# The order of the first unit's convolution, and more matmuls on zeros ahead of it

## The chip, the cores and the metric

The kernel runs on one core of one Trainium2 chip. A core has five engines that work side by side and wait for each other by semaphores: TensorE (PE, matrix products into the PSUM memory), VectorE (DVE), ScalarE (ACT), GpSimd (POOL) and SyncE (SP, which here only issues transfers). The metric is the device time of one execution in microseconds. The runs of the kernel before took 705.57 us in the median of three (705.44 to 706.24).

## The reference

```python
def _attn_ref(x, weight):             # x: (8, 4096, 192), weight: (8 heads, 7 taps)
    w = np.exp(weight - weight.max(-1, keepdims=True))
    w = w / (w.sum(-1, keepdims=True) + 1e-09)
    x_pad = np.concatenate([zeros(B, 6, 192), x], axis=1)
    x_unf = x_pad[:, idx, :].reshape(B, S, 7, 8, 24)      # idx[s, k] = s + k
    return np.einsum('hk,bskhg->bshg', w, x_unf).reshape(B, S, 192)

def _moe_ref(x, w_in, w_out):         # x: (32768, 192), w_in: (192, 2048), w_out: (2048, 192)
    h = x @ w_in
    return (h * np.cos(h)) @ w_out
```

So each token's 192 channels are first smoothed over the last seven tokens, with seven weights per head (24 channels each) that a softmax makes, and then go through a layer of 2048 hidden values with g = h cos h between two matrix products. Output and inputs are float32; the kernel multiplies in bfloat16 and adds up in float32.

## The kernel before, in words

The 32768 tokens are handled in units of 1024 tokens and tiles of 512 (two tiles a unit, 64 tiles). For a tile, the first product (`mm1`, L504) makes two blocks of 128 hidden values at a time in a PSUM tile `h` of two banks, eight times; ScalarE takes the cosine (L511), VectorE multiplies (L515) into `g`, and the second product (`mm2_step`, L553) adds 64 steps up in two PSUM banks `o_ps`. Three PSUM tiles `h` form a ring (`h_pool`), which the convolutions of the start use as well (`ring_banks`, `o_bank`). The order of TensorE's work within each tile is written out by hand (`PE_FIRST`, `PE_ORDER`), in program order per engine; an engine runs its instructions in that order and waits where an input is missing. The second product of tile 0 starts with the first `m1` in `PE_FIRST[0]`, after four of the eight `h` steps, `d11` and `h5`, `c11` (the convolution of unit 1 by a band matrix). `W0` and `W1` cast the two halves of w_out to bfloat16 on GpSimd (`cast_wo`, L123).

The first unit is convolved in another way, since nothing is at hand yet. Its eight blocks of 128 tokens form four pairs. `cast_first` (L396) casts two blocks of x. `turn_pair` (L406) turns one pair on TensorE with the identity matrix: six matmuls of 128 columns and six of 6 columns, so that channels lie on the partitions and tokens along the row; a copy takes the result to `xT`. `conv_pair` (L415) then adds up seven taps: for each tap j two matmuls, on the two halves of the rows, of a matrix that has the tap's weight on its diagonal (`diag`, made by `make_diag` from `wn`) with `xT` shifted by j tokens, 384 columns each. `conv_copy` (L424) takes one half of the result to `cT`, the left-hand input of the first product. Pairs 2 and 3 are convolved later, between the first products (`conv_later`, `v2` and `v3` in `PE_FIRST[0]`).

Around the change, the orders are these. TensorE: matmuls on zeros (`keep_warm`, 3 of them, L169), the weight's broadcast (L172), `WARM[0]` zeros (L173), the pick matmuls (L443), pair 0 turned (L444), `WARM[1]` zeros, pair 1 turned (L447), pair 0 convolved (L460), pairs 2 and 3 turned (L464), pair 1 convolved (L466), then the first product. ScalarE: casts of x, a table load for the sine, the copy of the turned pair 1, another cast, a copy of convolved pair 0, the copy of turned pairs 2 and 3, a copy of convolved pair 1. VectorE: the copy of turned pair 0, diagonals, `prod`, a copy of pair 0, `bands` (L468), a copy of pair 1. GpSimd: loads of w_in (L113, two early, two at L452), one cast of x, then 16 copies that put `bands` into the band matrix (L481), which unit 1's convolution needs, then unit 1's cast (L219) and w_out's.

SP's queue: unit 0 in three loads at the start; then a nop (L473) that waits for `m`, the second copy of pair 0 (VectorE's); behind it unit 1 in two loads (L103), its edges (L88), w_out in four loads (L127), then unit 2. So none of these is issued before `m` is done.

Of the kernel before, what the change touches and what calls it, by code (L numbers as in the profile page):

```python
# [16 lines left out]
def kernel(  # L17
# [8 lines left out]
    nc = tc.nc  # L26
# [5 lines left out]
    T = 512  # L32
# [9 lines left out]
    NC = D // 64  # L42
# [13 lines left out]

    CW = 2 * NPB * OP

    WARM, OUT = (2, 1), ((0, 1), (0, 1))
    xf = x.rearrange("b s d -> (b s) d")  # L60

    consts = ctx.enter_context(tc.tile_pool(name="consts", bufs=1))
# [72 lines left out]
    zero = consts.tile([128, T], BF16)  # L135
# [11 lines left out]
    nc.vector.memset(band, 0.0)  # L147
    idle = o_pools[0].tile([128, T], FP32, name="o_ps0")

    def keep_warm(n, bank=idle):  # L150
        for _ in range(n):
            nc.tensor.matmul(out=bank, lhsT=zero[:, 0:128], rhs=zero, start=True, stop=True)  # L152


    nc.gpsimd.affine_select(out=head, in_=head, compare_op=ALU.not_equal, fill=-1.0, base=0,
# [6 lines left out]
                          in_=bass.AP(ident.tensor, ident.offset, [ident[0:64].ap[0], [R, HQ], [HQ * R, 4], [0, 32]]))  # L162
# [4 lines left out]
    scrap = consts.tile([128, 1], FP32)  # L167
    nc.scalar.activation(out=scrap, in_=one, func=AF.Exp)
    keep_warm(3)  # L169
    w_all = o_pools[1].tile([128, T], FP32, name="o_ps1")  # L170
    w_bc = w_all[:, 0:K]
    nc.tensor.matmul(out=w_bc, lhsT=head, rhs=w_row, start=True, stop=True)  # L172
    keep_warm(WARM[0])  # L173

    wmax = consts.tile([128, 1], FP32)
# [65 lines left out]
    def ring_banks():  # L241
        h = h_pool.tile([128, 2, T], FP32, name="h")
        return [h[:, 0, :], h[:, 1, :]]
# [146 lines left out]
    EDGE = K - 1  # L390
    copies = [nc.scalar.copy, nc.vector.tensor_copy]
    cT[0] = cT_pool.tile([128, NC * (UB + 1) * 128], BF16, name="cT")
    xT = consts.tile([128, UB // 2, NC, EDGE + 128], BF16)
    diag = consts.tile([128, K, 2, 64], BF16)

    def cast_first(n0, n1, copy):  # L396
        copy(out=xb0[:, :, n0 + 1 : n1 + 1, :].rearrange("p k n m -> p n k m"),
             in_=x_tiles[0][:, n0:n1, :].rearrange("p n (m k) -> p n k m", k=NC))

    def make_diag(j0, j1):  # L400
        nc.vector.tensor_tensor(
            out=diag[:, j0:j1].rearrange("p j t m -> p j (t m)"),
            in0=double.rearrange("p (o t) m -> p o (t m)", o=1).to_broadcast([128, j1 - j0, 128]),
            in1=wn[:, j0:j1].rearrange("p (j o) -> p j o", o=1).to_broadcast([128, j1 - j0, 128]), op=ALU.mult)

    def turn_pair(p, ps):  # L406
        to = ps[:, 0 : NC * (EDGE + 128)].rearrange("p (k t) -> p k t", k=NC)
        for k in range(NC):
            for prev, t0, t1 in ((0, EDGE, EDGE + 128), (1, 0, EDGE)):
                n = 2 * p + 1 - prev  # L410
                nc.tensor.matmul(out=to[:, k, t0:t1], lhsT=xb0[:, k, n : n + 2, :].rearrange("p n m -> p (n m)"),  # L411
                                 rhs=ident[:, 128 - (t1 - t0) : 128], start=True, stop=True, skip_group_check=True)
        return to

    def conv_pair(p, ps, j0=0, j1=K):  # L415
        for j in range(j0, j1):
            for i in range(2):
                rows = slice(64 * i, 64 * i + 64)
                nc.tensor.matmul(out=ps[i][:, 0 : NC * 128].rearrange("p (k t) -> p k t", k=NC),  # L419
                                 lhsT=diag[rows, j].rearrange("p t m -> p (t m)"), rhs=xT[rows, p, :, j : j + 128],  # L420
                                 start=j == 0, stop=j == K - 1, skip_group_check=True)
        return ps

    def conv_copy(p, i, ps, copy):  # L424
        m = NC * (2 * p + i)
        return copy(out=cT[0][:, m * 128 : (m + NC) * 128], in_=ps[i][:, 0 : NC * 128])  # L426
# [10 lines left out]
    def o_bank(b):  # L437
        return o_pools[b].tile([128, T], FP32, name="o_ps%d" % b)
# [3 lines left out]
    for i in range(HQ):  # L442
        nc.tensor.matmul(out=wb[:, K * i : K * i + K], lhsT=pick[:, i], rhs=wn[0:64], start=i == 0, stop=i == HQ - 1, skip_group_check=True)  # L443
    to = [turn_pair(0, ring_banks()[0])]  # L444
    keep_warm(WARM[1])
    cast_first(2, 4, nc.scalar.copy)
    to.append(turn_pair(1, ring_banks()[0]))  # L447
    make_diag(0, 4)
    nc.vector.tensor_copy(out=xT[:, 0], in_=to[0])
    nc.scalar.activation(out=scrap, in_=one, func=AF.Sin)  # L450
# [8 lines left out]
                            in1=wb[:, 0 : HQ * K].rearrange("p (h o k) -> p h o k", o=1, k=K).to_broadcast([128, HQ, E, K]), op=ALU.mult)  # L459
    ps0 = conv_pair(0, [o_bank(0), ring_banks()[0]])  # L460
    conv_copy(0, 0, ps0, copies[0])
    m = conv_copy(0, 1, ps0, copies[1])
    rest = ring_banks()
    to = [turn_pair(2 + i, rest[i]) for i in range(2)]  # L464
    nc.scalar.copy(out=xT[:, 2:4], in_=bass.AP(to[0].tensor, to[0].offset, [to[0].ap[0], [T, 2], [1, NC * (EDGE + 128)]]))
    ps1 = conv_pair(1, [ring_banks()[0], o_bank(1)])  # L466
    bands = consts.tile([128, HQ, E], FP32)
    nc.vector.tensor_reduce(out=bands, in_=prod, axis=mybir.AxisListType.X, op=ALU.add)  # L468
    nc.gpsimd.tensor_copy(out=tap, in_=wn)
    conv_copy(1, 0, ps1, copies[0])  # L470
    conv_copy(1, 1, ps1, copies[1])

    tc.add_manual_dep(nc.sync.nop().ins, m.ins.name, sync_dep, reason="order of the transfers")  # L473
    load_unit(1, 0, NB)
# [4 lines left out]
    for i in range(16):  # L479
        q, rows = divmod(i, 4)  # L480
        nc.gpsimd.tensor_copy(out=band[32 * rows : 32 * rows + 32, HQ * q : HQ * (q + 1), 32 * rows : 32 * rows + E],  # L481
                              in_=bands[32 * q : 32 * q + 32])
# [244 lines left out]
```

## Time and profile before

| what | value |
|---|---|
| runs | 705.57 us median (705.44 to 706.24) |
| the profiled execution's own time | 706.02 us |
| its span, first to last instruction | 704.2 us |
| TensorE busy | 697.0 us, 99% of the span |
| VectorE, ScalarE, GpSimd busy | 91%, 91%, 72% |
| first convolution matmul (L419) | 5.91 us from the span's start |
| first matmul of the first product (L504) | 10.65 us |
| first matmul of the second product (L553) | 20.75 us |

Times in the profile are counted from the span's first instruction. A row of a timeline gives the start, the duration, the engine, the line in the kernel, the operation, what it writes and reads, the partitions and elements, and how many instructions were merged; in brackets stands how long the engine had been idle and what released it. A row of the waits gives who waited for whom, the total, how many times, and the longest. A row of the stretches gives the stretch, its length, the busy time of the engine, the granted clock, the transfer engines' share and the GB/s. A row of the transfers gives a queue with its packets, megabytes and share of the 16 transfer engines' time. Matmuls overlap in the engine's pipeline and their ends are modelled, so starts are the safer numbers.

### The profile page before, as it was taken

The page shows a single profiled execution, that of the slowest core. Times are in us where ns is not written, and L with a number is a line of the kernel's source. Part 1 is how long each engine was busy: PE and PEld are TensorE (multiplying, and loading weights), DVE is VectorE, ACT ScalarE, POOL GpSimd, SP SyncE. Part 2 cuts the span into 40 slices and gives each one's busy share as a digit, 9 for nine tenths or more (in the row PEclk, how much of TensorE's full clock was granted, in tenths as well). Part 3 has the DMA queues.
Part 4 walks back from the last instruction along what each step waited for, and adds up shares of the span by engine and source line. Part 5 has one row for each costly group of instructions (what it writes and reads, how often), then busy time and mean ns, then how long its engine had stood idle before and what let it go on. Part 6 is the DMA issues. An engine that isn't in the chain of part 4 may idle for free.

```text
span 704.2 us, 26828 instructions
## 1 busy us (share of the span) xinstructions
PE 697.0 (99%) x11832; PEld 531.5 (75%) x11832; DVE 642.5 (91%) x597; ACT 643.8 (91%) x830; POOL 505.0 (72%) x222
## 2 busy tenths in 40 slices
PE   8999999999999999999999999999999999999997
PEld 4677777777777777777777777777777777777776
DVE  6889999999999999999999999999999999999996
ACT  7889999999999999999999999999999999999875
POOL 6524478877779877778887778877789776899400
PEclk9999999999999999999999999999999999999999
DMA  8864466667567778576666687576665576874331
GB/s 201 227 164 97 111 139 152 122 152 170 131 157 141 133 151 177 132 158 122 150 154 147 153 158 122 147 164 148 144 149 131 144 175 136 153 127 95 92 91 47
DMA packets 227165, 99.69 MB, mean 142 GB/s; under 512 B 154729, under 2 KB 227049, under 8 KB 227049
## 3 DMA queue, kind: packets, MB, share of 16 engines
q1 hardware_dynamic: 225912, 97.01, 62.2%
q8 instruction: 92, 1.51, 0.9%
q0 software_dynamic: 832, 0.79, 0.8%
q14 instruction: 25, 0.20, 0.1%
q10 hardware_dynamic: 304, 0.20, 0.1%
HBM read 31.36 MB, written 25.17 MB: 80 GB/s over the span
## 4 chain that ended last, share of the span: by engine, by line
PE 97%; DMA 1%; SPq 0%; DVE 0%; POOL 0%; issue 0%; ACT 0%
PE o_ps L553 48%; PE h L504 47%; PE h L273 2%; DMA wo_f<-in_moe_w_out_dram 1%; PE h L553 0%; PE o_ps L419 0%; PE o_ps L152 0%; PE h L229 0%; POOL wo L123 0%; SPq L103 0%; PE h L411 0%; SPq L88 0%; DVE cT L426 0%; PE o_ps L172 0%; SPq L127 0%
## 5 line engine op out<-in xcount | busy, mean ns | idle before, releaser
L515 DVE TENSOR_TENSOR g<-h,cs 128x1024 bf16<-128x1024 f32 (+1 forms) x513 | 605.1, 1217 | 27.5 <-ACT cs L511 23.6
L511 ACT ACTIVATE cs<-h 128x1024 bf16<-128x1024 f32 (+1 forms) x513 | 511.0, 1021 | 44.5 <-PE h L504 30.9
L553 PEld LDWEIGHTS <-g 64*128 64x128 bf16 x8192 | 365.5, 94 | 92.3 <-issue 1.5
L553 PE MATMUL o_ps<-wo,g 64*128 64x192 bf16 x8128 | 426.3, 243 | 0.8 <-POOL wo L123 0.8
L504 PE MATMUL h<-cT,w 64*128 64x512 bf16 (+1 forms) x3078 | 412.3, 376 | 0.4 <-DVE cT L426 0.4
L504 PEld LDWEIGHTS <-w 64*128 64x128 bf16 x3078 | 160.5, 94 | 66.6 <-DVE cT L426 0.6
L212 POOL CAST xk<-x_f 128x768 bf16<-128x768 f32 (+1 forms) x56 | 76.4, 1366 | 114.0 <-DMA x_f<-in_x_dram 100.2
L353 POOL TENSOR_TENSOR raw_prod<-rT,tap 128x2784 f32<-128x2784 bf16 x28 | 135.3, 4832 | 0.2
L360 POOL TENSOR_TENSOR raw_prod<-raw_prod,pa 128x2088 f32<-128x2088 f32 x28 | 129.2, 4614 | 2.2
L345 ACT ACTIVATE pa<-rT,tap 128x348 f32<-128x348 bf16 x168 | 94.6, 580 | 0.0
L364 POOL TENSOR_TENSOR raw_prod<-raw_prod 128x1392 f32<-128x1392 f32 x28 | 87.9, 3138 | 2.2
L572 DVE COPY o_sb<-o_ps 128x384 f32<-128x384 f32 x62 | 34.6, 557 | 23.3 <-PE o_ps L553 23.2
L367 POOL TENSOR_TENSOR ro<-raw_prod 128x696 bf16<-128x696 f32 x28 | 46.4, 1659 | 2.2
L290 ACT CAST ct_buf<-h 112x480 bf16<-112x480 f32 x56 | 28.6, 562 | 4.1 <-PE h L273 0.4
L572 ACT COPY o_sb<-o_ps 128x384 f32<-128x384 f32 x64 | 30.7, 482 | 0.1
L273 PE MATMUL h<-xk,band 64*112 64x120 bf16 x448 | 21.8, 213 | 0.0
L273 PEld LDWEIGHTS <-band 64*112 64x112 bf16 x448 | 18.7, 127 | 0.0
L384 POOL COPY cT<-cT 128x144 bf16<-128x144 bf16 x3 | 0.9, 307 | 15.8 <-DMA cT<-ct 15.8
L303 POOL COPY ct<-ct 128x1728 bf16<-128x1728 bf16 x3 | 4.9, 1630 | 10.1 <-ACT ct L239 10.0
L219 POOL CAST x_bf<-x_f 128x1728 bf16<-128x1728 f32 (+2 forms) x4 | 7.8, 1966 | 0.1
L419 PE MATMUL o_ps<-xT,diag 64*128 64x384 bf16 x42 | 7.0, 366 | 0.2 <-DVE cT L426 0.2
L239 ACT CAST ct<-h 128x432 bf16<-128x432 f32 x12 | 5.9, 525 | 0.4 <-issue 0.4
(60 smaller groups left out, 60.2 us busy)
## 6 DMA issues: line engine op xcount, KB each, us to landing
out_dram<-o_sb SPq DMA_DIRECT2D x63, 384.0 KB, 4.5
x_f<-in_x_dram SPq DMA_DIRECT2D x28, 480.0 KB, 5.9
x_f<-in_x_dram SPq DMA_DIRECT2D x58, 192.0 KB, 2.7
cT<-ro SPq DMA_DIRECT2D x112, 87.0 KB, 2.3
wo_f<-in_moe_w_out_dram SPq DMA_DIRECT2D x4, 384.0 KB, 8.5
x_f<-in_x_dram SPq DMA_DIRECT2D x2, 768.0 KB, 9.6
x_f<-in_x_dram SPq DMA_DIRECT2D x3, 384.0 KB, 5.1
cT<-ct_buf SPq DMA_TRANSPOSE x56, 4.0
```

Of the source, the lines that this page charges most:

```text
L212: copy(out=xk[u][:, NC * n0 : NC * n1].rearrange("p (k n) m -> p k n m", k=NC), in_=x_tiles[u][:, n0:n1].rearrange("p n (m k) -> p k n m", ...
L273: return nc.tensor.matmul(out=ps[h // 4][0:OP, 0 : NPB * 4 * G].rearrange("p (m i r) -> p i m r", m=NC * NPB, i=4)[:, h % 4], lhsT=band[si ...
L345: mul(pa[u][:, j, part], tap_window(u, j)[:, part], tap[:, j : j + 1])
L353: nc.gpsimd.tensor_tensor(out=p, in0=tap_window(u, PA, K), in1=tap[:, PA:K].rearrange("p (j a b) -> p j a b", a=1, b=1).to_broadcast([128, ...
L360: add(out=p[:, 0:m], in0=p[:, 0:m], in1=a[:, done : done + m], op=ALU.add)
L364: add(out=p[:, 0:m], in0=p[:, 0:m], in1=p[:, n - m : n], op=ALU.add)
L367: add(out=ro[u], in0=p[:, 0], in1=p[:, 1], op=ALU.add)
L504: nc.tensor.matmul(out=h[:, i, n0 * 128 : n1 * 128], lhsT=w[rows, k, j, :], rhs=rhs, start=(k == 0), stop=(k == NC - 1))
L511: nc.scalar.activation(out=cs[:, :, part], in_=h[:, :, part], func=AF.Sin, bias=math.pi / 2.0, scale=1.0)
L515: nc.vector.tensor_tensor(out=g_tiles[t][:, 2 * j : 2 * j + 2, part], in0=h[:, :, part], in1=cs[:, :, part], op=ALU.mult)
L553: ms.append(nc.tensor.matmul(out=o_ps[tt, b, si], lhsT=g_tiles[tt][rows, f, s * 128 : (s + 1) * 128], rhs=wo[rows, f // 2, f % 2, :], star ...
L572: (copy or copies[b])(o_sb[t][:, 2 * b : 2 * b + 2, :].rearrange("p s d -> p (s d)"), o_ps.pop((t, b)))
```

## The change

Three things are edited. `WARM` grows from (2, 1) to (3, 2, 3): three zero matmuls of 512 columns instead of two behind the weight's broadcast, two of 128 columns instead of one of 512 between the two turned pairs, and three of 128 columns, new, behind the second turned pair. `keep_warm` gets the number of columns. And pairs 0 and 1 are convolved one right after the other; pairs 2 and 3 are turned behind them, each in a ring tile of its own, and copied to `xT` by two instructions (one on ScalarE, one on VectorE) instead of one on ScalarE, behind the copies of pair 1. `m`, for which the nop on SP waits, becomes the second copy of pair 1. `bands` stands behind all of that on VectorE.

```diff
-    WARM, OUT = (2, 1), ((0, 1), (0, 1))
+    WARM, OUT = (3, 2, 3), ((0, 1), (0, 1))
...
-    def keep_warm(n, bank=idle):
+    def keep_warm(n, bank=idle, cols=T):
         for _ in range(n):
-            nc.tensor.matmul(out=bank, lhsT=zero[:, 0:128], rhs=zero, start=True, stop=True)
+            nc.tensor.matmul(out=bank[:, 0:cols], lhsT=zero[:, 0:128], rhs=zero[:, 0:cols], start=True, stop=True)
...
     to = [turn_pair(0, ring_banks()[0])]
-    keep_warm(WARM[1])
+    keep_warm(WARM[1], cols=128)
     cast_first(2, 4, nc.scalar.copy)
     to.append(turn_pair(1, ring_banks()[0]))
+    keep_warm(WARM[2], cols=128)
     make_diag(0, 4)
...
     ps0 = conv_pair(0, [o_bank(0), ring_banks()[0]])
     conv_copy(0, 0, ps0, copies[0])
-    m = conv_copy(0, 1, ps0, copies[1])
-    rest = ring_banks()
-    to = [turn_pair(2 + i, rest[i]) for i in range(2)]
-    nc.scalar.copy(out=xT[:, 2:4], in_=bass.AP(to[0].tensor, to[0].offset, [to[0].ap[0], [T, 2], [1, NC * (EDGE + 128)]]))
+    conv_copy(0, 1, ps0, copies[1])
     ps1 = conv_pair(1, [ring_banks()[0], o_bank(1)])
+    to = [turn_pair(2 + i, ring_banks()[0]) for i in range(2)]
+    conv_copy(1, 0, ps1, copies[0])
+    m = conv_copy(1, 1, ps1, copies[1])
+    nc.scalar.copy(out=xT[:, 2], in_=to[0])
+    nc.vector.tensor_copy(out=xT[:, 3], in_=to[1])
     bands = consts.tile([128, HQ, E], FP32)
     nc.vector.tensor_reduce(out=bands, in_=prod, axis=mybir.AxisListType.X, op=ALU.add)
     nc.gpsimd.tensor_copy(out=tap, in_=wn)
-    conv_copy(1, 0, ps1, copies[0])
-    conv_copy(1, 1, ps1, copies[1])
```

## The prediction

> **What bounds the kernel now.** I read the page first, then the waits of TensorE over the whole run, then the chain that ended last, then each engine's timeline of the first 20 us. The page says which engine carries the span:
>
> ```profile
> span 704.2 us, 26828 instructions
> PE 697.0 (99%) x11832; PEld 531.5 (75%) x11832; DVE 642.5 (91%) x597; ACT 643.8 (91%) x830; POOL 505.0 (72%) x222
> ```
>
> TensorE is idle for 7 us in all. Where? The waits of TensorE after 20 us hold one entry, and the busy time in two later stretches shows that nothing else is lost there:
>
> ```profile
> PE o_ps L553 <- POOL wo L123: 0.8, 1, 0.8
> ...
> 21.00:50.00 29.00, 29.00 (x473) 1.00 0.73 179
> ...
> 100.00:690.00 590.00, 590.00 (x10154) 1.00 0.65 141
> ```
>
> From 21 us on TensorE runs without a hole, on work that the change doesn't touch. So the end is set by when TensorE gets past that wait, the first matmul of the second product (L553), which needs the first half of w_out as bf16. The chain (start, duration, what) leads back from there:
>
> ```profile
> 8.01 0.32 PE o_ps L419
> ...
> 8.39 0.57 DVE cT L426
> ...
> 8.98 0.37 SPq L103
> ...
> 9.39 0.51 SPq L103
> ...
> 9.94 0.79 SPq L88
> ...
> 10.79 0.41 SPq L127
> ...
> 11.24 7.93 DMA wo_f<-in_moe_w_out_dram
> ...
> 19.23 1.48 POOL wo L123
> ...
> 20.75 0.26 PE o_ps L553 x2
> ```
>
> The reader is to see that the transfers hang on one copy. The nop at L473 holds SP's queue until VectorE's copy of a convolved pair (8.39 to 8.96) is done; then unit 1, its edges and w_out are issued in that order, w_out lands at 19.17, GpSimd casts it in 1.48 us, and TensorE goes on at 20.75. Whatever TensorE, ScalarE or VectorE do earlier between 9 and 20 us ends in a longer wait at 20.75. The gate moves only if SP's release moves, or if another input of that stage becomes later than w_out.
>
> **The change part by part.** First the order that sets the release. The nop waited for the second copy of pair 0; after the change `m` is the second copy of pair 1. So one has to know how fast two pairs in a row are convolved. TensorE's timeline (start, duration, idle before in brackets):
>
> ```profile
> 1.34 1.46 PE L152 MATMUL o_ps<-zero 128*128 128x512 bf16 x3 [1.34 <-DVE zero L136]
> ...
> 3.25 1.03 PE L152 MATMUL o_ps<-zero 128*128 128x512 bf16 x2
> 4.46 0.19 PE L443 MATMUL o_ps<-wn,pick 64*128 64x7 bf16 x2 [0.18 <-DVE wn L186]
> ...
> 5.00 0.59 PE L152 MATMUL o_ps<-zero 128*128 128x512 bf16 x1
> 5.39 0.59 PE L411 MATMUL h<-ident,x_bf 128*128 128x128 bf16 x6
> 5.91 0.50 PE L419 MATMUL o_ps<-xT,diag 64*128 64x384 bf16 x1
> ...
> 7.80 0.52 PE L419 MATMUL o_ps<-xT,diag 64*128 64x384 bf16 x1
> ...
> 8.26 0.96 PE L411 MATMUL h<-ident,x_bf 128*128 128x128 bf16 x12
> 9.15 0.50 PE L419 MATMUL h<-xT,diag 64*128 64x384 bf16 x1
> ...
> 9.77 0.38 PE L419 MATMUL h<-xT,diag 64*128 64x384 bf16 x1
> ...
> 9.99 0.32 PE L419 MATMUL h<-xT,diag 64*128 64x384 bf16 x1
> ...
> 10.15 0.32 PE L419 MATMUL h<-xT,diag 64*128 64x384 bf16 x1
> ...
> 10.65 0.49 PE L504 MATMUL h<-cT,w 64*128 64x256 bf16 x6
> ```
>
> A tap is two matmuls side by side. From 5.91 to 7.80 there are six steps, 0.315 us each; from 9.99 to 10.15 a step is 0.16 us. So TensorE's clock doubles between 9.77 and 9.99, although the column of the granted clock reads 1.00 all the way. When it doubles after the change decides most of what follows.
>
> The zero matmuls. Three of 512 columns take 1.46 us and one 0.59, so one more costs 0.435 us, and one of 128 columns a quarter, 0.11. The third at L173 fills the 0.18 us before 4.46 and pushes the pick matmuls from 4.46 to about 4.55. Two short ones for one long save 0.21: turning pair 1 starts near 5.29 (5.39 before). Twelve turning matmuls take 0.89 (8.26 to 9.15), so six take 0.45, and three short zeros 0.33: TensorE is free at 6.07. The other input of the convolution is VectorE's copy of the turned pair 0, whose row stands with the others' that I use:
>
> ```profile
> 5.18 0.58 DVE L449 CAST xT<-h 128x402 bf16<-128x402 f32 x1
> ...
> 8.87 0.70 DVE L468 TENSOR_REDUCE bands<-prod 128x76 f32<-128x532 bf16 x1
> ...
> 6.54 0.48 ACT L454 CAST xT<-h 128x402 bf16<-128x402 f32 x1
> ```
>
> It ends at 5.76, and 0.1 later after the change, so about 6.05 is the new start, against 5.91: a cost of 0.15 us on the path. Pair 1's input from ScalarE is ready at 7.02, before pair 0 is through in any case below 7 cold steps (6.05 + 2.2 = 8.25) or at a doubling near 6.7 (7.5).
>
> Two pairs are 14 steps. With the doubling at time F, (F - 6.05)/0.315 of them are slow, the rest take 0.164. What sets F? In the rows, TensorE's last named idle stretch before the doubling ends at 4.46, 5.3 us ahead of 9.8. The change closes that hole, so matmuls then follow on from 1.34. If 5.3 us of matmuls without a hole are what it takes, F is 6.7: 2.1 slow steps, 11.9 fast ones of 1.95 us, last column at 8.65. If the hole had no part, F stays at 9.8: 11.9 slow, 2.1 fast, last column at 10.15. I take 6.7: the added 0.54 us of zeros lie in just that stretch.
>
> [...]
>
> From last column to copy: 8.39 less the end of the last slow step (7.80 + 0.315 = 8.12) is 0.27, about 0.23 at full clock. The copy takes 0.56. So SP is released at 8.65 + 0.23 + 0.56 + 0.03 = 9.47 instead of 8.98: 0.5 us later. What is behind it: unit 1, its edges, w_out, unit 2, all on SP's queue in that order.
>
> Does w_out land 0.5 us later? The queues' share of the transfer engines from 5.5 to 10, 10 to 12 and 12 to 19 us:
>
> ```profile
> q0 software_dynamic: 609, 0.58, 90.5%
> ...
> q0 software_dynamic: 190, 0.17, 62.6%
> q1 hardware_dynamic: 250, 0.19, 37.5%
> ...
> q1 hardware_dynamic: 2979, 2.22, 106.2%
> ```
>
> q0 is w_in (GpSimd's loads), q1 is SP's. The engines are full without a break: with w_in to about 11.5, then with SP's. A release 0.5 us later leaves the slots of 10 to 11 to w_in, which then ends sooner. So the landing is late by between 0 (all of it filled) and 0.5 (none filled). I take 0.2, nearer the filled end, since SP's queue had only 37.5% of the two microseconds in question. [...]
>
> Cast and gate follow the landing: +0.2 us at 20.75.
>
> The second half, turned behind both pairs, drops out: one copy of two pairs on ScalarE becomes one on ScalarE and one on VectorE, and the first product starts near 9.2 instead of 10.65. One more tile of the PSUM ring is taken than before; the readers of the reused ones are the copies of the turned pairs (7.02 at the latest) and of pair 0 (8.3), all done when they are written again. I cost this part at nothing, gain or loss, covered by the wait for w_out. What could uncover it is the band matrix: its reduction (8.87) now stands behind VectorE's copies of pair 1 and of the turned pair 3. The first ends at 9.45, the second takes 0.58, so the reduction starts at about 10.0, 1.15 late. Behind it:
>
> ```profile
> 9.63 4.52 POOL L481 CAST band<-bands 32x76 bf16<-32x76 f32 x16 [1.35 <-DVE bands L468]
> 14.21 2.70 POOL L219 CAST x_bf<-x_f 128x768 bf16<-128x768 f32 x2
> ...
> 17.36 0.54 PE L229 MATMUL h<-x_bf,band 128*128 128x216 bf16 x4
> ...
> 18.39 0.94 ACT L239 CAST ct<-h 128x432 bf16<-128x432 f32 x2
> ...
> 19.37 0.53 PE L229 MATMUL h<-x_bf,band 128*128 128x216 bf16 x4 [0.61 <-ACT ct L239]
> ```
>
> GpSimd ends unit 1's cast at 18.05 instead of 16.91, still ahead of w_out at 19.4. TensorE's convolution of unit 1 goes from 17.36 to 18.1, ScalarE's copies end near 19.6, and the second convolution ends near 20.2, ahead of the gate at 20.95. So the slack of 0.85 at 20.75 shrinks to about 0.75, and nothing is paid.
>
> Sum: 0.2 us. The profiled execution took 706.02 us, 1.8 outside its span of 704.2; the median of the runs is 705.57, 0.45 below it. On the median: 705.57 + 0.2 = 705.8.
>
> **The rivals.**
>
> Slower: the clock doubles no earlier than before. SP is then released at 10.15 + 0.23 + 0.56 + 0.03 = 10.97, 2.0 us late. w_in is through by 11.5, so the engines stand empty for part of it. What SP's queue moved before its new start is lost: 37.5% of 2 us is 0.75, and some 0.2 of full rate after 12. So w_out is late by 0.95 at the least, by 2.0 if nothing fills in: 706.5 to 707.6, with 706.8 as my value. It passes 0.2%, which is 1.4 us and about what a measurement of this kernel tells from no change, where less than 0.6 of those 2.0 us are filled. For it: between 4.46 and 9.8 the rows show hardly a hole, and still the clock stayed down. Against it: the hole at 4.46 is the one that the change fills.
>
> Slower by another mechanism: the band matrix comes later than I count. The slack is 0.75 us; every further 0.1 at the reduction is 0.1 at 20.75. With a reduction 2 us late and w_out on time it costs 0.1 to 0.5: 706.1. Against it: a late reduction and a late w_out have the same cause, so w_out hides it.
>
> Faster: the wait for w_out is less fixed than the chain has it, and the earlier first product (1.45 us) reaches the end. TensorE's idle at the gate is 0.85 us in all, so at most that: 704.7. Against it: the releaser of that wait is GpSimd's cast, and w_out cannot land sooner while its issue comes later.
>
> **How the numbers follow.** Forecast 0.58, unmoved clock 0.30, late band 0.06, faster 0.06. Over 0.2% slower: half of the second, a third of the third, and 0.03 of the forecast, 0.20. Over 0.2% faster: half of the last and 0.02 of scatter, 0.05. Within: 0.75. The runs of before spread by 0.8 us (705.44 to 706.24), so the low end is 705.57 less that, 704.8; the high end takes in the unmoved clock but for its last third, 707.3. The forecast's own range is 705.0 to 706.4.
>
> **What would show it.** Right: steps of 0.16 us from about the third tap on, SP's first transfer after the nop at 9.3 to 9.6, w_out landing at 19.2 to 19.5, the first product from about 9.2, and a longer wait of TensorE at L553. Wrong: steps of 0.315 into the second pair and SP's release near 11; a wait at L553 on anything but GpSimd's cast of w_out; w_out landing a full microsecond off; or holes in TensorE after 21 us.

## The result, and the profile after

The changed kernel took 707.73 us in the median of 22 runs (705.81 to 709.2), the kernel before 705.78 beside it. The ratio is 1.0021, with a 95% interval of 1.0012 to 1.0029: about 1.5 us slower. (It is not the ratio of the two medians, which lie 1.95 us apart; the ratios below are of the same kind.) The forecast was 705.8, its range 704.8 to 707.3 and its likeliest outcome "within 0.2%".

The profiled execution has a span of 706.4 us, 2.2 longer than before. The page and TensorE's longest wait over the whole run:

```profile
span 706.4 us, 26838 instructions
...
PE 698.7 (99%) x11837; PEld 531.0 (75%) x11837; DVE 643.2 (91%) x598; ACT 643.4 (91%) x830; POOL 504.9 (71%) x222
...
PE h L229 <- POOL x_bf L219: 2.4, 1, 2.4
```

The wait for w_out's cast is gone from the list. TensorE now waits for unit 1's cast, 2.35 us at once. The chain that ended last, in its first 23 us (start, duration, what), tells why that cast is late:

```profile
8.47 0.29 PE o_ps L419
...
10.46 0.56 DVE cT L426
11.03 0.58 DVE xT L469
11.60 0.62 DVE bands L471
...
12.28 0.24 POOL band L482
...
16.52 0.25 POOL band L482
...
16.83 1.21 POOL x_bf L219
...
18.12 1.47 POOL x_bf L219
19.64 0.71 PE h L229 x4
20.34 1.39 PE h L505 x4
21.73 0.84 PE h L229 x4
22.57 0.27 PE o_ps L554 x2
```

Before, this chain ran through SP's queue and w_out. Now VectorE's copies of pair 1 and of the turned pair 3 stand ahead of the bands' reduction, which starts at 11.52 instead of 8.87; GpSimd's 16 copies into the band matrix and its cast of unit 1 follow, and TensorE can convolve unit 1 only from 19.64 (17.36 before). The reduction's row before and after:

```profile
8.87 0.70 DVE L468 TENSOR_REDUCE bands<-prod 128x76 f32<-128x532 bf16 x1
```

```profile
11.52 0.70 DVE L471 TENSOR_REDUCE bands<-prod 128x76 f32<-128x532 bf16 x1
```

w_out was in time, though its cast too starts 1.14 us later than before:

```profile
20.37 1.47 POOL L123 CAST wo<-wo_f 128x1536 bf16<-128x1536 f32 x1 [0.79 <-DMA wo_f<-in_moe_w_out_dram]
```

It ends at 21.84, ahead of 22.50, where the second product starts (20.75 before). One thing more is in that chain: the first product's step at 20.34 takes 1.39 us. In the timeline, where the merged row counts six matmuls, it is 0.82 before and 1.46 after:

```profile
17.94 0.82 PE L504 MATMUL h<-cT,w 64*128 64x512 bf16 x6
```

```profile
20.28 1.46 PE L505 MATMUL h<-cT,w 64*128 64x512 bf16 x6
```

The stretches of TensorE (stretch, its length, busy time, granted clock, then the transfers) show that its granted clock read 0.50 for 3.42 us, and 1.00 ahead of it:

```profile
16.43:19.84 3.41, 1.06 (x12) 1.00 1.10 326
19.84:23.26 3.42, 3.42 (x20) 0.50 1.08 317
```

So the 2.2 us are 1.75 at the start of the second product, and the 0.76 us after it at half rate, 0.4. In this execution w_out alone would have held the second product until 21.84, 1.1 us later than before; the bands and the half clock add the other half.

TensorE's timeline at the start shows where the two pairs in a row were slow:

```profile
5.83 0.48 PE L152 MATMUL o_ps<-zero 128*128 128x128 bf16 x3
6.37 0.47 PE L419 MATMUL o_ps<-xT,diag 64*128 64x384 bf16 x1
...
9.20 0.52 PE L419 MATMUL h<-xT,diag 64*128 64x384 bf16 x1
...
9.52 0.37 PE L419 MATMUL h<-xT,diag 64*128 64x384 bf16 x1
...
9.73 0.32 PE L419 MATMUL h<-xT,diag 64*128 64x384 bf16 x1
```

The convolution starts at 6.37 (5.91 before), and the clock doubles near 9.6 (a step takes 0.32 us up to 9.52 and 0.16 to 0.17 from 9.73 on), 0.3 us sooner than before and not 3. The first product starts at 10.95, 0.3 us later than before.

### The profile page after: what moved, and what is told of

The parts are those of the page before. It is cut to its first block, busy times and chain, and to the rows that moved or that the text cites. A ratio compares the mean times of both kernels' runs of the same rounds, so it can differ in the third digit from the quotient of the medians.

```text
span 706.4 us, 26838 instructions
## 1 busy us (share of the span) xinstructions
PE 698.7 (99%) x11837; PEld 531.0 (75%) x11837; DVE 643.2 (91%) x598; ACT 643.4 (91%) x830; POOL 504.9 (71%) x222
## 4 chain that ended last, share of the span: by engine, by line
PE 98%; POOL 1%; DVE 0%; issue 0%; POOLq 0%
PE o_ps L554 48%; PE h L505 47%; PE h L273 2%; POOL band L482 1%; PE h L229 0%; PE o_ps L152 0%; POOL x_bf L219 0%; PE h L554 0%; PE o_ps L419 0%; PE h L419 0%; PE h L411 0%; DVE bands L471 0%; DVE xT L469 0%; DVE cT L426 0%; PE o_ps L172 0%
```

## The experiments

After the profile my theory was: the change makes two inputs late, w_out (by the late release) and unit 1's cast (by the late bands); the second opens the hole, and the hole halves the clock. The rival was that the late release alone makes the time. The first four runs are a square of the two causes, and a filled hole. The results give a mean granted clock for each execution. A lost window, below, is a stretch of 3.41 or 3.42 us at a granted clock of 0.50, as in the profile above. The three profiled executions that have one show a mean clock of 0.997, 0.998 and 0.998, the other eleven 0.999 or 1.0; so I count the executions at 0.998 or less as having one. Of the 22 of the changed kernel 17 have it; their spans have a median of 706.0 us, those of the other five 704.2. The 1.8 between them is about what 3.41 us at half rate lose, 1.7. Of the kernel before, 3 of 35 had it beside the first four runs, 4 of 35 beside the next four, and 1 of 44 beside the last four.

**The bands' reduction put back, nothing else.**

```diff
     conv_copy(0, 1, ps0, copies[1])
+    bands = consts.tile([128, HQ, E], FP32)
+    nc.vector.tensor_reduce(out=bands, in_=prod, axis=mybir.AxisListType.X, op=ALU.add)
     ps1 = conv_pair(1, [ring_banks()[0], o_bank(1)])
...
-    bands = consts.tile([128, HQ, E], FP32)
-    nc.vector.tensor_reduce(out=bands, in_=prod, axis=mybir.AxisListType.X, op=ALU.add)
```

> The changed kernel with the reduction of the bands back in its old place, behind the copy of pair 0 on VectorE; nothing else. Theory (two late inputs: SP's late release makes w_out 1.1 us late, the late band matrix makes unit 1's convolution later still, and the hole of 2.35 us on TensorE that it opens halves the clock for 3.4 us): GpSimd's copies into the band matrix start near 10.1 instead of 12.28, unit 1 is cast by 17.5, no hole above 1.5 us, no half clock, and the wait for w_out is the gate again at 21.9: 1.1 us over the kernel before. Rival (the late release alone makes the time, and the band only fills a wait that is there anyway): 2.2 us over it in the profile, as the changed kernel.

Measured: 706.23 us against 706.01, ratio 1.0004 (0.9993 to 1.0014); 3 of 12 executions with a lost window. Most of the loss is gone. In the profile the band copies start at 10.04, the hole is 1.39 us and w_out is the gate again, as expected; but at 20.56, not 21.9, and there the theory was off. SP is released at 10.54 there, 1.6 us later than before, and w_out's cast starts no later. Unit 1's cast ends at 18.11 and not by 17.5, since GpSimd waits 0.81 us for the second part of its transfer. The rows of SP's first two loads behind the nop and of the cast:

```profile
10.54 0.92 SPq L103 DMA_DIRECT2D x_f<-in_x_dram  x2
...
19.04 1.47 POOL L123 CAST wo<-wo_f 128x1536 bf16<-128x1536 f32 x1 [0.92 <-DMA wo_f<-in_moe_w_out_dram]
```

**The release put back, nothing else** (`m` is the second copy of pair 0 again).

```diff
-    conv_copy(0, 1, ps0, copies[1])
+    m = conv_copy(0, 1, ps0, copies[1])
...
-    m = conv_copy(1, 1, ps1, copies[1])
+    conv_copy(1, 1, ps1, copies[1])
```

> The changed kernel with the nop on SP waiting for the second copy of pair 0 again; nothing else. Theory of two late inputs: w_out lands 1.6 us or so sooner, near 18.8, but the band matrix is as late as before, so TensorE still waits for unit 1's cast until 19.6, the clock still halves, and the second product still starts near 22.5: no better than the changed kernel by more than 0.2 us. Rival (late release alone): back to the kernel before, within 0.3 us.

Measured: 707.22 us, ratio 1.0013 (1.0003 to 1.0022); 7 of 12 with a lost window. In its profile TensorE waits 2.24 us for unit 1's cast and not at all for w_out, as the theory has it. But unit 1's convolution starts at 18.66 and the second product at 20.69, not near 19.6 and 22.5: the clock doubled sooner there, near 7.8, and it was not halved later, which is taken up below.

**Both put back.** The two diffs above together.

> Both put back: bands behind the copy of pair 0 and the nop waiting for that copy; the zeros and the order on TensorE stay changed. Theory of two late inputs: second product near 20.7, as in the kernel before, time within 0.5 us of it. A third view, that the order on TensorE or the zeros cost something of themselves: 1 us or more over the kernel before.

Measured: 706.08 us, ratio 0.9997 (0.9987 to 1.0007); 1 of 12 with a lost window. So TensorE's new order and the zeros cost nothing that shows. The profile is of the one execution with the lost window, and there the hole of 3.10 us is not the bands': GpSimd has them by 13.71 and waits 1.43 and 1.17 us for the two parts of unit 1's transfer:

```profile
9.19 4.52 POOL L482 CAST band<-bands 32x76 bf16<-32x76 f32 x16 [0.80 <-DVE bands L465]
15.14 1.21 POOL L219 CAST x_bf<-x_f 128x768 bf16<-128x768 f32 x1 [1.43 <-DMA x_f<-in_x_dram]
17.52 1.46 POOL L219 CAST x_bf<-x_f 128x960 bf16<-128x960 f32 x1 [1.17 <-DMA x_f<-in_x_dram]
```

The square, in ratios: late bands add 0.0017 with the late release (1.0004 to 1.0021) and 0.0016 without it (0.9997 to 1.0013), 1.1 to 1.2 us; the late release adds 0.0008 and 0.0007, some 0.5 us. Each ratio is uncertain by 0.001, so the first is shown and the second is not told from nothing. With the second measurement of the changed kernel further down, 1.0015, the late bands add 0.0011 with the late release and the late release 0.0002 with the late bands; that the bands cost then rests on the other row and on the counts of lost windows.

**Zeros in the hole**: in `PE_FIRST[0]`, ten zero matmuls of 512 columns ahead of unit 1's first convolution.

```diff
-K1 h0a h0b h1 v2 h2 h3 v3 W0 h4 d11 h5 d21 W1 c11 m1 ...
+K1 h0a h0b h1 v2 h2 h3 v3 W0 h4 w10 d11 h5 d21 W1 c11 m1 ...
```

> The changed kernel with ten zero matmuls of 512 columns put on TensorE ahead of unit 1's first convolution, where it waits 2.35 us: 2.15 us of them at full clock. Nothing is sooner on any other engine. If the half clock is a cost of its own, the convolution still starts near 19.6, but the steps to the second product take 2.2 us instead of 2.9 or end on w_out at 21.9, and what follows runs at full clock: 0.8 to 1.1 us less than the changed kernel. If the clock is not what makes it slow, no gain.

Measured: 706.85 us against 706.01, ratio 1.0008 (0.9999 to 1.0016); none of 11 with a lost window, the longest span 705.7 us. TensorE's timeline there:

```profile
16.25 2.33 PE L152 MATMUL o_ps<-zero 128*128 128x512 bf16 x9
19.08 0.53 PE L229 MATMUL h<-x_bf,band 128*128 128x216 bf16 x4 [0.50 <-POOL x_bf L219]
19.54 0.82 PE L505 MATMUL h<-cT,w 64*128 64x512 bf16 x6
```

(Nine of the ten have a record.) The convolution starts at 19.08, half a microsecond sooner than expected, since the clock doubled near 7.6 there; the step behind it is back at 0.82 us. The zeros give no engine anything sooner, and the long executions are gone: the half clock is a cost of its own. How much of the 1.5 us it is, the run doesn't settle. By the ratios it is 0.9 against the first measurement and 0.5 against the second one further down, and the zeros hold back executions whose unit 1 would have been ready sooner.

**The order alone, with the zeros of before** (`WARM = (2, 4, 0)`: 512 columns in all between the turned pairs, none behind).

> The changed kernel's order with the zeros of the kernel before (two of 512 columns behind the broadcast, 512 columns in all between the turned pairs, none behind): the order alone. Theory (the late band matrix opens a hole on TensorE and the hole halves the clock; when the clock doubles at the start is a matter of the execution): the convolution starts 0.3 to 0.4 us sooner, the doubling falls anywhere between 6.5 and 10 us, most executions lose a clock window as in the changed kernel: ratio 1.001 to 1.0025. Rival (the zeros are what makes the clock double early where it does): more executions with a half clock than the changed kernel's 17 of 22, and slower than it by 0.3 us or more.

Measured: 707.26 us against 706.33, ratio 1.0006 (0.9996 to 1.0017); 6 of 11 with a lost window. The rival is out: without the added zeros there are not more long executions but, if anything, fewer. The ratio is below the 1.001 that the theory had at the least. And the profile, of an execution with a lost window, shows a second late input: GpSimd has the band matrix by 15.69 and waits 1.35 us more for unit 1's transfer.

**The zeros alone**, in the kernel before:

```diff
-    WARM, OUT = (2, 1), ((0, 1), (0, 1))
+    WARM, OUT = (3, 2, 3), ((0, 1), (0, 1))
...
+    keep_warm(WARM[2], cols=128)
```

> The kernel before with the changed kernel's zeros alone. Theory: the convolution starts 0.4 us later, nothing else moves; the bands stay early, so the hole stays short and few executions lose a clock window: within 0.4 us of the kernel before (ratio 0.9995 to 1.0006). Rival (the zeros cost): 0.5 us or more over it. Rival (the zeros help): 0.4 us or more under it.

Measured: 706.36 us against 706.33, ratio 1.0002 (0.9991 to 1.0014); 2 of 11. They neither cost nor help in that order as far as this shows. The first convolution matmuls of the two, the order alone and the zeros alone:

```profile
5.91 0.50 PE L419 MATMUL o_ps<-xT,diag 64*128 64x384 bf16 x1
```

```profile
6.37 0.47 PE L419 MATMUL o_ps<-xT,diag 64*128 64x384 bf16 x1
```

So the zeros put the start off by 0.46 us; a gain from it shows in neither run's time.

**The bands' reduction right behind its product**, ahead of `conv_pair(0, ...)`, in the changed kernel: the same two lines moved up by three more.

> The changed kernel with the reduction of the bands right behind their product on VectorE, ahead of the copy of pair 0, where VectorE waits 1.8 us for TensorE. The band matrix then waits for neither convolution and GpSimd's copies start near 8.4. Theory: unit 1's cast then waits for its transfer alone, few executions with a half clock; median within 0.4 us of the kernel before. If unit 1's transfer, which SP releases late, takes the band's place as the late input, half clocks stay in a third of the executions or more and the time is 0.5 us over the kernel before.

Measured: 706.42 us against 706.33, ratio 1.0 (0.9988 to 1.0012); 3 of 11 with a lost window. The hole is 1.49 us in the profile, and GpSimd now waits for unit 1's transfer (1.07 and 1.17 us). So a late transfer is next in line behind the bands, without a cost that shows in the median.

**The kernel before with the bands' reduction early and zeros in its three waits** (`w2` ahead of `d11`, `c11` and `m1`).

> The kernel before with the bands reduced right behind their product, and two zero matmuls of 512 columns (0.43 us) ahead of each of TensorE's three waits before the second product. Theory: the zeros lie in waits and cost nothing where w_out is the gate; no execution loses a clock window, where 3 of 35 do in the kernel before: median the same or up to 0.3 us less, highest run below 707. If the zeros push unit 1's convolutions past the landing of w_out: 0.3 to 0.9 us slower.

Measured: 706.78 us against 706.33, ratio 1.0003 (0.9992 to 1.0013); 1 of 12 with a lost window. Nothing is won: one execution lost its window all the same (span 706.7), and the highest run was 708.75, not below 707.

**SP released 5 us sooner**: the changed kernel with the bands' reduction right behind the product, and `m` the copy of the turned pair 0.

```diff
-    nc.vector.tensor_copy(out=xT[:, 0], in_=to[0])
+    m = nc.vector.tensor_copy(out=xT[:, 0], in_=to[0])
```

> The changed kernel with the bands reduced right behind their product and the nop on SP waiting for VectorE's copy of the turned pair 0, so SP is released near 6 instead of 11. It asks what the late release is worth by itself. If the transfer engines, full with w_in until 11.5, set when w_out lands (landing moved 19.7, 19.0, 18.8 for releases at 8.5, 10.5, 9.0 in the runs so far), w_out lands no sooner than 18.5, w_in lands later, and the time is within 0.5 us of the kernel before. If the release sets it, w_out lands 2 us or more sooner and the second product starts before 19: 1 to 2 us less than the kernel before, unless the first product now waits for w_in, which costs the same again.

Measured: 705.33 us against 705.89, ratio 0.9994 (0.9985 to 1.0002); none of 11 with a lost window. SP is released at 6.00 and w_out's cast starts at 18.03:

```profile
6.00 0.92 SPq L103 DMA_DIRECT2D x_f<-in_x_dram  x2
...
18.03 1.47 POOL L123 CAST wo<-wo_f 128x1536 bf16<-128x1536 f32 x1 [2.10 <-DMA wo_f<-in_moe_w_out_dram]
```

Against the run with the bands put back that is 4.5 us sooner at the release and 1.0 at the cast: between these two traces the release moves w_out by a fifth or so of itself, more than the first expectation (none before 18.5) and far less than the second. The fifth is no rule: with SP released at 9.94 (the second trace of the changed kernel) and at 9.96 (the order alone) w_out's cast starts at 18.75 and at 20.41. No run here says where that scatter comes from.

**w_out first**, in the kernel before with the early bands: the first half of w_out is loaded ahead of unit 1 and cast first; unit 1's convolution goes behind the first product on TensorE, and its copies likewise on ScalarE (that line and the bands are left out below).

```diff
+    load_wo(0)
     load_unit(1, 0, NB)
...
-    load_wo(0)
...
-"K1 h0a h0b h1 v2 h2 h3 v3 W0 h4 d11 h5 d21 W1 c11 m1 h6 m11 h7 L2 c21 D1"
+"W0 K1 h0a h0b h1 v2 h2 h3 v3 h4 m2 h5 m4 h6 W1 m4 h7 L2 m2 d11 d21 c11 c21 D1"
```

> The kernel before with the bands reduced early, the first half of w_out loaded ahead of unit 1, cast first, and unit 1's convolution moved behind the first product of tile 0 on TensorE, with the second product's steps spread between. If the wait for w_out and for unit 1's cast are what TensorE loses there (0.6 and 0.85 us of holes), w_out lands near 16, the holes before 21 us go and the time falls by 0.8 to 1.5 us. If ScalarE and VectorE set the pace of the first tile (1.0 and 1.2 us for each of its eight steps), the holes move to the ring of PSUM tiles and the time stays within 0.4 us, or rises where unit 1 becomes late.

Measured: 706.29 us against 705.89, ratio 1.0007 (0.9997 to 1.0017). The second expectation holds, at its edge (within 0.4 us: the medians lie 0.40 apart). w_out's cast starts at 16.19, and TensorE waits elsewhere: for VectorE's products, which free the PSUM ring.

```profile
PE h L229 <- DVE g L515: 0.8, 2, 0.6
PE o_ps L553 <- POOL wo L123: 0.4, 1, 0.4
PE o_ps L553 <- DVE cT L426: 0.4, 1, 0.4
```

**The changed kernel once more**, and the early release with the zeros of before.

> The changed kernel once more, beside the others on one chip. Theory (late band matrix, hole, half clock): half or more of its executions with a mean clock of 0.998 or less, those 1.5 us or so longer than the rest; the rest level with the kernel before; ratio 1.001 to 1.003.

Measured: 706.99 us against 705.89, ratio 1.0015 (1.0004 to 1.0026); 6 of 12 executions with a lost window, median span 705.9, the other six 704.05, level with the kernel before (704.1). As expected.

> As the run with SP released by the turned pair 0 and the bands reduced early, with the zeros of the kernel before, so the convolution starts at 5.9 instead of 6.4. If the early release, the early bands and the absence of half clocks are what made that run 0.56 us shorter in the median than the kernel before, this one is 0.5 to 0.9 us shorter, no execution with a half clock. If that was scatter: within 0.3 us.

Measured: 705.22 us against 705.88, ratio 0.9994 (0.9985 to 1.0003); 1 of 11 with a lost window. Two variants with the early release and the early bands thus lie 0.56 and 0.66 us under the kernel before; each interval reaches 1, so that they beat it is likely and not shown.

Counted together, the runs with the late bands lost a window in 36 of 57 executions (the changed kernel twice, the release put back, the order alone), those with the changed kernel's order and early bands in 8 of 57. Of these 8, 6 fell in the 23 executions that kept the late release.

## Why the prediction was right or wrong

**Right: what bounds it.** TensorE stayed without a hole behind the second product's start (busy for 25.00 us of 25 to 50, and for 640.00 of 50 to 690), so what that start waits for sets the time.

**Not shown: the release's price.** SP was released not 0.5 us late but 2.06 in the profile (11.04 against 8.98) and 0.96 in the second trace of the changed kernel. The cast of w_out, for which the sum has 0.2, started 1.14 us later than before in the one and 0.48 us sooner in the other (18.75 against 19.23). The square puts the late release at some 0.5 us, not told from nothing, where the rival of the unmoved clock had 0.95 to 2.0 for 2.0 us. So the release was cheap, but the 0.2 is neither shown nor refuted. The first product's start, forecast near 9.2, was 10.95 and 9.85 in the two traces, so an earlier one was hardly put to the test.

**Wrong: the doubling at 6.7.** The step read "if 5.3 us of matmuls without a hole are what it takes, F is 6.7". The change did close the hole ahead of the pick matmuls, and in the profiled execution the clock still doubled near 9.6. In seven traces TensorE runs the same instructions up to the doubling (the changed kernel twice, the first four experiments and the early release), and it comes near 9.6 and 7.4, 8.6, 7.8, 6.8, 7.6, and 6.7. The run with both put back, where it comes within two taps:

```profile
6.37 0.47 PE L419 MATMUL o_ps<-xT,diag 64*128 64x384 bf16 x1
...
6.64 0.43 PE L419 MATMUL o_ps<-xT,diag 64*128 64x384 bf16 x1
...
6.91 0.32 PE L419 MATMUL o_ps<-xT,diag 64*128 64x384 bf16 x1
```

So it is a matter of the execution, over some 3 us. In the three traces with a half clock (the changed kernel, both put back, the order alone) the clock reads 0.50 from 19.84, 20.50 and 21.50 on, 10.24, 13.65 and 13.65 us behind the doubling: three and four times the 3.41 us that the half clock lasts. The doubling should have been a spread, instead of one F.

In all fourteen traces, with the added zeros or without, the doubling lies between 6.70 us (the early release) and 9.88 (the kernel before). Whether the hole ahead of the pick matmuls holds it back stays open: the five traces in which TensorE waits there (0.2 us for `wn`) have the doubling between 7.8 and 9.88, the nine others between 6.70 and 9.6.

The start at 6.05 has a slip of its own: a zero of 0.435 us that fills a hole of 0.18 pushes the pick matmuls by 0.26, by the difference, and not by 0.09; in the trace it was 0.19 (4.65 against 4.46).

**Wrong, and this is what decided: "I cost this part at nothing".** The prediction had the reduction 1.15 us late and the slack at 0.75, both from F at 6.7 and a start at 6.05. The reduction was 2.65 late in the profile, from the later doubling, a start 0.3 later than reckoned, and the copies in a row on VectorE; unit 1's convolution started 2.28 us late, and the slack was gone. The rival of the late band named this mechanism, with 0.06 and 0.1 to 0.5 us, on the argument that w_out would be as late and hide it. It was late, but not as late: w_out's cast ended at 21.84, the second product started at 22.50. Over the runs, the square gives the late bands 1.1 to 1.2 us, most of the loss (0.8 with the second measurement), and the counts of lost windows, 36 against 8 of 57, say the same.

**Missing: a hole can halve the clock.** No step priced what a hole does to the work behind it. Below, for four more traces, the stretch of 3.41 us that holds most of the hole, and the next one. For the traces without a half clock the edges are my estimate, in steps of 3.41 us from the doubling, after the 10.24 and 13.65 of the other three. With both put back, then the order alone (here with the stretch before):

```profile
17.08:20.50 3.42, 1.28 (x10) 1.00 1.10 326
20.50:23.91 3.41, 3.32 (x26) 0.50 1.09 304
```

```profile
14.67:18.08 3.41, 1.66 (x19) 1.00 0.98 305
18.08:21.50 3.42, 1.50 (x13) 1.00 0.94 281
21.50:24.91 3.41, 3.41 (x32) 0.50 1.02 300
```

The release put back, and the changed kernel once more:

```profile
14.67:18.08 3.41, 1.75 (x19) 1.00 1.07 317
18.08:21.49 3.41, 2.55 (x24) 1.00 1.10 327
```

```profile
14.19:17.60 3.41, 2.04 (x21) 1.00 0.98 300
17.60:21.01 3.41, 2.30 (x22) 1.00 1.10 332
```

With TensorE busy for 1.06 (the changed kernel's profile above), 1.28 and 1.50 us of such a stretch the clock of the next one reads 0.50; with 1.66, 1.75 and more it reads 1.00, in every such stretch of the fourteen traces from the doubling to 24 us. The hole with the release put back, 2.24 us, is nearly as long as the changed kernel's 2.35, but an edge, as estimated, cuts it in two. If the busy time of such a stretch is what counts, where the edges lie decides with the hole's length whether a window is lost. That would account for the changed kernel's two groups of spans, at 704.2 and 706.0; its two traces differ in both (holes of 2.35 and 1.88 us), so it is not shown there. Nor do the other traces show it: the lengths of the holes alone sort them as well, 2.35, 3.10 and 3.39 us with a half clock behind them, 2.24 at the most without. The edges of the undisturbed traces are reckoned and not seen, and a limit between 1.50 and 1.66 us is what these traces fit, not more.

What opens the hole is not always the band matrix. It is in both traces of the changed kernel and with the release put back; with both put back and with the order alone unit 1's transfer came last. So early bands make lost windows rarer and don't end them.

**The end of the forecast.** "Within 0.2%" had 0.75 and slower 0.20; the measured 0.21% lies on that bound, its interval on both sides of it. The median of 707.73 lies above the range's 707.3; the ratio, taken on the 705.57 that the forecast started from, gives 707.05, inside it. That is luck: the range reaches so far because it took in the unmoved clock at the rival's price for w_out, and the time came from the bands and a half clock that no term had. Of the two slower rivals it was the one that I gave 0.06 that made the time, in the profiled execution set off by the other's late doubling.

## What to carry to other kernels

When an instruction is moved behind others on its engine, follow its own chain to the point where it is needed, at the latest start that the rows allow and not at the likeliest: here a 0.7 us reduction nobody seemed to wait for led to 16 copies, a cast and a convolution. A wait on TensorE can cost more than its length, as here, where 3.42 us at half clock followed on 2.35 us of waiting; look at the clock of the work behind it. And where executions fall into two groups, count them by a number that the results give for each (here the mean clock) before explaining a median.

## What the runs showed of the hardware that was not expected

Behind a hole of 2.35 us on TensorE the granted clock read 0.50 for 3.42 us (19.84 to 23.26 in the changed kernel's profile). With zeros in the hole none of 11 executions lost a window.

The column of the granted clock reads 1.00 ahead of the first doubling (at 9.88 us in the kernel before, near 9.6 in the changed one), while the steps there take 0.315 us instead of 0.16: before that point only the durations told the clock.
